# GpSimd's weight additions in quarters of 128 columns: a delta-rule attention and a gated layer on one core

## The chip, the core and the metric

The kernel runs on one NeuronCore of a Trainium2 chip. Five engines work side by side, each through its own queue in order: TensorE (PE, matrix products into PSUM), VectorE (DVE), ScalarE (ACT), GpSimd (POOL), and SyncE (SP), which here issues nearly all transfers. They meet only through semaphores. SBUF is the on-chip memory, PSUM the memory that PE writes. The metric is device time in microseconds (us) of one execution.

## The reference: what is computed

```python
state = np.zeros((B, H, D, D), dtype=np.float32)      # B, H, S, D = 4, 8, 768, 48
for t in range(S):
    kt, vt, bt = (k_n[:, :, t], v[:, :, t], beta[:, :, t, None])
    y[:, :, t] = np.einsum('bhd,bhde->bhe', q[:, :, t], state)
    v_old = np.einsum('bhde,bhd->bhe', state, kt)
    state = state + bt[:, :, :, None] * np.einsum('bhd,bhe->bhde', kt, vt - v_old)
...
h = x @ w_in            # x is y as 3072 x 384, w_in 384 x 2048
g = h * np.cos(h)
return (g @ w_out).astype(np.float32)                 # w_out 2048 x 384
```

`k_n` is `k` divided by its norm. All inputs and the output are fp32.

## The kernel before

The sequence of 768 steps is cut into 24 units of 32 steps. Within a unit, the recurrence becomes a triangular solve: PE transposes k and q (`turn`, L594), forms the products of keys with keys and queries (`gram`, L625), the triangular matrix is inverted, PE multiplies the right side by the inverse (`solve`, L897), and updates the state (`update`, L920, added by DVE at L928). For the first four units the inverse is made by elimination of 16x16 halves: PE spreads rows (`rows`, L707), and L727 and L734 multiply and subtract. Units 0 and 1 are eliminated by DVE, units 2 and 3 together by GpSimd. ACT then puts the result in place (`unfold`, L742), and PE uses it in two halves (`solve_half` and `between`, both L864). From unit 4 on the inverse is made on GpSimd by substitution (`invert`, L797 and L804), goes out through DRAM (L808) and comes back (L817). k's norms are a power on GpSimd (L541), scaled on DVE (L552 to L557).

Two units give 64 steps of 4 batches, that is 256 tokens, for the gated layer. The first two pairs use plain products (`hidden`, L980, of 12 matmuls of 128x128x128; `output`, L1181), later ones a scheme with fewer products (L1158, L1246) whose weight sums are formed from the same weights.

The weights are used in a reduced form that is prepared on the chip. `w_in` is cut into twelve blocks of 128 rows by 512 columns (`narrows[0]` to `narrows[11]`: four column groups, three row groups each), `w_out` into sixteen of 128 by 384. Each block t passes through one of six stages in `in_sum` and `w_sum` (t modulo 6): a load by SP (L489), two passes on ACT that split each word (L497, L499), two on DVE (L503 with two operands in SBUF, L508 with one), and an addition of 32-bit integers on GpSimd (`narrow_add`, L512) that writes the block in its final place. SP may load block t + 6 when the addition of block t is done; a hidden product waits for the additions of the three blocks that it reads, an output product for those of `w_out`.

The order of the work is written out by hand: every piece is a task with an engine, dependencies and buffers (`add(key, engine, ...)`), and `Order.LINE` lists the numbers of all tasks in the order in which they are emitted. `Order.OTHER` names the tasks that run on the second of two possible engines. Every engine thus has a fixed order; there is no scheduler. On GpSimd, the additions stand in this order: blocks 2, 0, 1 in one train, then 3, later 5, 4, 6, each between scalings of v (`weigh`, L582), then 7; 10 and 8 stand inside the elimination of units 2 and 3, 9 and 11 after it, with additions of `w_out` blocks around them.

Small filler matmuls (`heat`, L1194) stand on PE in the first 65 us.

Of the kernel before, what the change touches and what calls it, by code (L numbers as in the profile page):

```python
# [12 lines left out]
U32 = mybir.dt.uint32  # L13
ALU = mybir.AluOpType
# [35 lines left out]
class Order:  # L50

    OTHER = {
        ('weigh', 0, 0), ('unfold', 0), ('weigh', 0, 1), ('fold', 1), ('unfold', 1),
        ('weigh', 1, 0), ('fold', 2), ('weigh', 1, 1), ('unfold', 2), ('unfold', 3),
        ('right', 4, 0), ('left', 1, 2, 0), ('x_sum', 2, 'd'), ('x_sum', 2, 'n'),
        ('x_sum', 2, 'm'), ('x_sum', 2, 'e'), ('x_sum', 2, 'k'), ('x_sum', 2, 'g'),
        ('x_sum', 2, 'i'), ('x_sum', 2, 'l'), ('x_sum', 2, 'f'), ('x_sum', 2, 'h'),
        ('x_sum', 2, 'b0'), ('left', 2, 2, 0), ('x_sum', 3, 'd'), ('x_sum', 3, 'n'),
        ('x_sum', 3, 'm'), ('x_sum', 3, 'e'), ('x_sum', 3, 'k'), ('x_sum', 3, 'g'),
        ('x_sum', 3, 'i'), ('x_sum', 3, 'l'), ('x_sum', 3, 'f'), ('x_sum', 3, 'h'),  # L60
        ('x_sum', 3, 'b0'), ('left', 3, 1, 0), ('left', 3, 4, 1), ('left', 3, 3, 0),
        ('x_sum', 4, 'd'), ('x_sum', 4, 'n'), ('x_sum', 4, 'm'), ('x_sum', 4, 'e'),
        ('x_sum', 4, 'k'), ('x_sum', 4, 'g'), ('x_sum', 4, 'l'), ('x_sum', 4, 'f'),
        ('x_sum', 4, 'h'), ('x_sum', 4, 'b0'), ('left', 4, 4, 0), ('left', 4, 3, 0),
        ('left', 4, 3, 1), ('x_sum', 5, 'd'), ('x_sum', 5, 'm'), ('x_sum', 5, 'e'),
        ('x_sum', 5, 'i'), ('x_sum', 5, 'f'), ('x_sum', 5, 'h'), ('left', 5, 2, 0),
        ('left', 5, 4, 0), ('left', 5, 4, 1), ('left', 5, 3, 0), ('x_sum', 6, 'd'),
        ('x_sum', 6, 'e'), ('x_sum', 6, 'l'), ('x_sum', 6, 'f'), ('x_sum', 6, 'h'),
        ('x_sum', 6, 'b0'), ('left', 6, 2, 1), ('left', 6, 4, 0), ('left', 6, 3, 0),
        ('x_sum', 7, 'd'), ('x_sum', 7, 'n'), ('x_sum', 7, 'm'), ('x_sum', 7, 'g'),  # L70
        ('x_sum', 7, 'i'), ('x_sum', 7, 'h'), ('left', 7, 1, 0), ('left', 7, 2, 0),
        ('left', 7, 2, 1), ('left', 7, 4, 0), ('left', 7, 3, 1), ('x_sum', 8, 'd'),
        ('x_sum', 8, 'm'), ('x_sum', 8, 'e'), ('x_sum', 8, 'k'), ('x_sum', 8, 'f'),
        ('x_sum', 8, 'h'), ('x_sum', 8, 'b0'), ('left', 8, 4, 1), ('left', 8, 3, 0),
        ('x_sum', 9, 'n'), ('x_sum', 9, 'e'), ('x_sum', 9, 'k'), ('x_sum', 9, 'i'),
        ('x_sum', 9, 'b0'), ('left', 9, 2, 0), ('left', 9, 1, 1), ('left', 9, 4, 0),
        ('left', 9, 4, 1), ('left', 9, 3, 0), ('left', 9, 3, 1), ('x_sum', 10, 'd'),
        ('x_sum', 10, 'n'), ('x_sum', 10, 'e'), ('x_sum', 10, 'g'), ('x_sum', 10, 'l'),
        ('x_sum', 10, 'f'), ('x_sum', 10, 'h'), ('x_sum', 10, 'b0'), ('left', 10, 1, 0),
        ('left', 10, 1, 1), ('left', 10, 4, 0), ('left', 10, 3, 0), ('x_sum', 11, 'f'),  # L80
        ('x_sum', 11, 'b0'), ('left', 11, 1, 0), ('left', 11, 2, 0), ('left', 11, 2, 1),
        ('left', 11, 4, 0), ('left', 11, 4, 1),
# [139 lines left out]
def kernel(  # L222
# [287 lines left out]
    def narrow_add(t):  # L510
        w = narrows[t][0].bitcast(U32)
        nc.gpsimd.tensor_tensor(out=w, in0=w, in1=words.pop(t)[:, :, 0], op=ALU.add)  # L512
# [1315 lines left out]
```

## Time and profile before

| | us |
|---|---|
| median of 3 runs | 644.84 (644.37 to 646.28) |
| the profiled execution's own time | 644.59 |
| its span, first to last instruction | 642.8 |
| PE busy | 613.6 (95%) |
| DVE busy | 505.4 (79%) |
| POOL busy | 447.9 (70%) |
| ACT busy | 263.3 (41%) |

The profile gives for each engine its busy time, for each instruction its start and length, and for idle time the event that ended it. Groups of instructions are named by line of the kernel, engine and operation, then the tile written and the tiles read, and the shape as partitions x elements. In a timeline, the first column is the start in us from the span's begin and the second the length; `[3.61 <-DVE u_half L882]` says that the engine stood idle for 3.61 us before it, until an instruction of DVE at L882. Like instructions in a row are merged (x3). The granted clock is TensorE's, as a share of full speed. The spans of instructions on POOL are rough.

### The profile page before, as it was taken

The numbers are of one execution on the slowest core, as the hardware profiler recorded it, in microseconds if no ns is written. First come the engines' busy times: TensorE is split into PE (matmuls) and PEld (weight loads), VectorE is DVE, ScalarE is ACT, GpSimd is POOL, SyncE is SP. The second block draws the span as 40 slices with busy tenths as digits, with TensorE's granted clock in tenths as the row PEclk, the third lists the DMA queues.
The fourth block names the chain that finished last, engine by engine and source line by source line (L and its number), as shares of the span: only waits on it lengthen the run. The fifth ranks groups of instructions, "written<-read, shape, count | busy, mean of one in ns | idle before, by whom it ended". The sixth has DMA issues, their size and how long they took to land.

```text
span 642.8 us, 28246 instructions
## 1 busy us (share of the span) xinstructions
PE 613.6 (95%) x12316; PEld 572.7 (89%) x12316; DVE 505.4 (79%) x955; ACT 263.3 (41%) x467; POOL 447.9 (70%) x783
## 2 busy tenths in 40 slices
PE   5677999999999999999998999999999999999997
PEld 4566888886999989999998999999999999999997
DVE  7896887599999888789788778777778867556582
ACT  3535565822233631533523533622633433435340
POOL 4465899888888788787888886885897874152032
PEclk9677999999999999999999999999999999999999
DMA  6884475554453542635535404425304202000000
GB/s 122 217 215 133 102 197 140 123 93 70 75 96 51 100 76 40 115 64 99 89 42 98 86 7 84 74 53 101 67 2 85 51 2 34 28 2 26 2 25 25
DMA packets 202924, 50.01 MB, mean 78 GB/s; under 512 B 194544, under 2 KB 197760, under 8 KB 202800
## 3 DMA queue, kind: packets, MB, share of 16 engines
q1 hardware_dynamic: 201536, 47.82, 37.5%
q8 instruction: 97, 1.59, 1.1%
q10 hardware_dynamic: 1088, 0.20, 0.2%
q0 software_dynamic: 176, 0.18, 0.2%
q14 instruction: 27, 0.22, 0.1%
HBM read 38.19 MB, written 9.96 MB: 75 GB/s over the span
## 4 chain that ended last, share of the span: by engine, by line
PE 87%; DVE 7%; DMA 1%; issue 1%; POOL 1%; ACT 1%; SPq 0%; DVEq 0%; POOLq 0%
PE p_out L1246 29%; PE p_h L1158 28%; PE p_h L980 7%; PE p_kq L834 4%; PE p_out L1181 3%; PE p_u L897 3%; PE p_g L625 3%; PE p_s L920 3%; PE p_kq L937 3%; PE p_o L1246 2%; PE p_z L956 1%; DVE rows L734 1%; PE p_t L594 1%; DVE rows L727 1%; DVE g_ffn L1175 1%
## 5 line engine op out<-in xcount | busy, mean ns | idle before, releaser
L797 POOL TENSOR_TENSOR part<-z,gb 128x126 f32<-128x126 f32 (+22 forms) x310 | 138.8, 448 | 39.9 <-DMA gb<-g_dr 7.9
L804 POOL TENSOR_TENSOR z<-z,part 128x126 f32<-128x126 f32 (+22 forms) x310 | 145.8, 470 | 24.3
L1246 PE MATMUL p_out<-w_out,g_ffn 128*128 128x192 f32 x672 | 121.6, 329 | 2.0 <-DVE o L1298 1.8
L1246 PEld LDWEIGHTS p_out<-w_out,g_ffn 128*128 128x128 f32 x672 | 107.8, 190 | 3.7 <-issue 2.2
L1037 ACT ACTIVATE turns<-turns,halfpi 128x512 f32<-128x512 f32 x96 | 68.4, 720 | 78.7 <-DVE turns L1028 78.3
L1262 POOL TENSOR_TENSOR g_ffn<-g_ffn 128x512 f32<-128x512 f32 x37 | 49.0, 1329 | 67.3 <-DVE g_ffn L1040 46.0
L1246 PE MATMUL p_out<-w_sum,g_ffn 128*128 128x192 f32 x496 | 90.1, 329 | 0.4 <-DVE o L1298 0.4
L1158 PE MATMUL p_h<-x_sum,w_in 128*128 128x128 f32 x640 | 83.0, 277 | 0.3 <-DVE g_ffn L1175 0.3
L1246 PEld LDWEIGHTS p_out<-w_sum,g_ffn 128*128 128x128 f32 x496 | 79.5, 190 | 1.4 <-DVE o L1298 0.6
L1158 PEld LDWEIGHTS p_h<-x_sum,w_in 128*128 128x128 f32 x640 | 77.8, 192 | 1.7 <-DVE g_ffn L1175 0.6
L1021 ACT ACTIVATE turns<-g_ffn,quarter_turn 128x512 int32<-128x512 f32 x70 | 49.2, 719 | 59.8 <-DVE g_ffn L1175 38.9
L1175 DVE TENSOR_TENSOR g_ffn<-g_ffn,p_h 128x512 f32<-128x512 f32 x80 | 54.1, 679 | 24.6 <-PE p_h L1158 23.6
L1028 DVE SCALAR_TENSOR_TENSOR turns<-g_ffn,turns 128x512 f32<-128x512 f32 x70 | 55.8, 805 | 15.1 <-ACT turns L1021 14.9
L1040 DVE TENSOR_TENSOR g_ffn<-turns,g_ffn 128x512 f32<-128x512 f32 x70 | 50.9, 736 | 12.7 <-ACT turns L1037 12.6
L1158 PE MATMUL p_h<-x_sum,in_sum 128*128 128x128 f32 x400 | 54.0, 278 | 0.3 <-issue 0.3
L1158 PEld LDWEIGHTS p_h<-x_sum,in_sum 128*128 128x128 f32 x400 | 49.3, 191 | 1.5 <-issue 0.4
L980 PE MATMUL p_h<-x_ffn,w_in 128*128 128x128 f32 x384 | 48.3, 285 | 0.0
L980 PEld LDWEIGHTS p_h<-x_ffn,w_in 128*128 128x128 f32 x384 | 45.7, 198 | 1.0 <-issue 0.2
L1262 DVE TENSOR_TENSOR g_ffn<-g_ffn 128x512 f32<-128x512 f32 x51 | 44.3, 872 | 1.6 <-PE p_out L1246 1.5
L541 POOL TENSOR_TENSOR knrm<-ksum,halves 128x16 f32<-128x16 f32 (+1 forms) x14 | 38.8, 2768 | 9.0 <-DVE ksum L529 7.9
L1298 DVE SCALAR_TENSOR_TENSOR o<-p_out,o 128x192 f32<-128x192 f32 x74 | 25.0, 350 | 24.5 <-PE p_out L1246 23.8
L1170 ACT COPY p_h<-p_h 128x512 f32<-128x512 f32 x40 | 23.0, 574 | 48.9 <-PE p_h L1158 33.6
(145 smaller groups left out, 1052.9 us busy)
## 6 DMA issues: line engine op xcount, KB each, us to landing
gb<-g_dr SPq DMA_DIRECT2D x20, 256.0 KB, 4.1
vp<-in_v_dram SPq DMA_DIRECT2D x96, 48.0 KB, 3.0
in_sum<-in_moe_w_out_dram SPq DMA_DIRECT2D x12, 384.0 KB, 3.3
out_dram<-o SPq DMA_DIRECT2D x23, 192.0 KB, 2.5
in_sum<-in_moe_w_in_dram SPq DMA_DIRECT2D x8, 512.0 KB, 5.3
kp<-in_k_dram SPq DMA_DIRECT2D x128, 24.0 KB, 2.2
z_dr<-z SPq DMA_DIRECT2D x10, 256.0 KB, 3.6
zt<-z_dr SPq DMA_DIRECT2D x80, 32.0 KB, 2.4
```

The source lines that it names most:

```text
L541: nc.gpsimd.tensor_tensor(out=scales[m][2][:, part], in0=sums[m, part.start][:, 0:n], in1=halves[:, 0:n], op=ALU.pow,)
L797: nc.gpsimd.tensor_tensor(out=part, in0=z[:, 0:rows, j, None].to_broadcast(shape), in1=a[:, j, None, j + 1 :].to_broadcast(shape), op=ALU. ...
L804: nc.gpsimd.tensor_tensor(out=behind, in0=behind, in1=part, op=ALU.subtract)
L980: nc.tensor.matmul(p_h[:, i], w_in[:, t, (4 * k + i) * 128 : (4 * k + i + 1) * 128], xts[p][:, t, unit * 128 : (unit + 1) * 128], start=(i ...
L1021: nc.scalar.activation(turns[p, f], hidden_of(p, f), AF.Identity, bias=quarter_turn, scale=TURN)
L1028: nc.vector.scalar_tensor_tensor(out=r, in0=hidden_of(p, f), scalar=TURN, in1=t, op0=ALU.mult, op1=ALU.subtract,)
L1037: nc.scalar.activation(r, r, AF.Sin, bias=halfpi, scale=2.0 * math.pi)
L1040: nc.vector.tensor_tensor(out=place(p, f), in0=step_of(rests.pop((p, f)), f), in1=step_of(hidden_of(p, f), f), op=ALU.mult,)
L1158: nc.tensor.matmul(p_h[:, e], in_block(*w)[:, e], x_of(p, b), start=new and e == 0, stop=True, skip_group_check=True,)
L1175: nc.vector.tensor_tensor(out=part_of(p, to), in0=part_of(p, one), in1=part_of(p, two), op=op)
L1246: nc.tensor.matmul(p_o, left(p, part, a)[:, e % 4], right(e, b), start=(e == 0), stop=(e == FT // 2 - 1), skip_group_check=True,)
L1262: either(("left", p, x, s), nc.vector, nc.gpsimd).tensor_tensor(out=left(p, s, to), in0=left(p, s, one), in1=left(p, s, two), op=op)
```

## The change

Each addition of a `w_in` block on GpSimd becomes four additions of 128 columns, in the order of the columns, directly behind one another. The sixteen additions of `w_out` blocks stay whole. The last quarter keeps the key of the old task, so what depends on the block in the task list still depends on its last quarter; in the instructions, each matmul that reads a quarter waits for that quarter. In `LINE` 36 numbers are added and the others renumbered; `OTHER` holds the same 120 keys in another sequence. Leaving the quarters out, the order on every engine is the same as before.

```diff
     OTHER = {
...
     LINE = """
...
-    def narrow_add(t):
-        w = narrows[t][0].bitcast(U32)
-        nc.gpsimd.tensor_tensor(out=w, in0=w, in1=words.pop(t)[:, :, 0], op=ALU.add)
+    PIECES = 4
+
+    def narrow_add(t, piece, pieces):
+        w, lo = narrows[t][0].bitcast(U32), words[t][:, :, 0]
+        n = narrows[t][2] // pieces
+        cols = slice(piece * n, piece * n + n)
+        nc.gpsimd.tensor_tensor(out=w[:, cols], in0=w[:, cols], in1=lo[:, cols], op=ALU.add)
+        if piece == pieces - 1:
+            words.pop(t)
...
         add(("shift", t), "DVE", 1.4 * c, lambda: narrow_shift(t), [("split", t)])
-        add(("add", t), "POOL", 1.45 * c, lambda: narrow_add(t), [("shift", t)],
+        deps, pieces = [("shift", t)], PIECES if t < 12 else 1
+        for i in range(pieces - 1):
+            add(("part", t, i), "POOL", 0.5, lambda i=i: narrow_add(t, i, pieces), deps)
+            deps = [("part", t, i)]
+        add(("add", t), "POOL", 1.45 * c / pieces, lambda: narrow_add(t, pieces - 1, pieces), deps,
             due=W_IN + 2 * t if t < 12 else W_OUT + 2 * (t - 12))
```

More of the change, by code (lines that the diff above doesn't have):

```diff
@@ L52 @@
     OTHER = {
[L53 to L82, printed above, removed]
+        ('weigh', 0, 0), ('unfold', 1), ('left', 7, 4, 0), ('x_sum', 8, 'h'), ('left', 9, 3, 0),
@@ new lines @@
+        ('x_sum', 4, 'b0'), ('x_sum', 11, 'f'), ('left', 7, 3, 1), ('left', 5, 4, 0),
+        ('x_sum', 3, 'e'), ('x_sum', 2, 'l'), ('x_sum', 7, 'd'), ('left', 4, 3, 1),
+        ('left', 4, 4, 0), ('x_sum', 3, 'm'), ('x_sum', 3, 'k'), ('fold', 2), ('left', 6, 3, 0),
+        ('unfold', 3), ('x_sum', 7, 'n'), ('left', 1, 2, 0), ('unfold', 0), ('x_sum', 7, 'h'),
+        ('x_sum', 5, 'e'), ('left', 9, 4, 1), ('x_sum', 4, 'l'), ('x_sum', 6, 'f'),
+        ('left', 7, 1, 0), ('x_sum', 3, 'b0'), ('x_sum', 5, 'm'), ('x_sum', 10, 'f'),
@@ new lines @@
+        ('x_sum', 2, 'd'), ('x_sum', 9, 'n'), ('left', 7, 2, 1), ('x_sum', 7, 'i'),
+        ('x_sum', 8, 'f'), ('x_sum', 2, 'n'), ('x_sum', 4, 'g'), ('left', 4, 3, 0),
+        ('x_sum', 2, 'h'), ('x_sum', 4, 'd'), ('x_sum', 10, 'g'), ('unfold', 2),
+        ('x_sum', 9, 'i'), ('x_sum', 3, 'l'), ('left', 10, 4, 0), ('x_sum', 4, 'n'),
+        ('left', 2, 2, 0), ('x_sum', 2, 'i'), ('x_sum', 4, 'h'), ('left', 9, 1, 1),
+        ('left', 3, 3, 0), ('x_sum', 6, 'e'), ('left', 5, 4, 1), ('x_sum', 11, 'b0'),
@@ new lines @@
+        ('left', 10, 1, 0), ('left', 3, 1, 0), ('x_sum', 10, 'e'), ('x_sum', 3, 'd'),
+        ('x_sum', 8, 'e'), ('left', 10, 3, 0), ('x_sum', 3, 'n'), ('x_sum', 7, 'g'),
+        ('x_sum', 6, 'b0'), ('x_sum', 3, 'h'), ('x_sum', 8, 'm'), ('left', 5, 2, 0),
+        ('left', 11, 1, 0), ('x_sum', 8, 'k'), ('x_sum', 2, 'f'), ('x_sum', 5, 'd'),
+        ('left', 3, 4, 1), ('x_sum', 10, 'b0'), ('weigh', 1, 1), ('left', 11, 2, 1),
+        ('x_sum', 3, 'i'), ('x_sum', 8, 'b0'), ('x_sum', 5, 'h'), ('x_sum', 4, 'f'),
@@ new lines @@
+        ('x_sum', 2, 'g'), ('left', 8, 3, 0), ('left', 6, 2, 1), ('x_sum', 6, 'l'),
+        ('x_sum', 4, 'k'), ('left', 11, 4, 1), ('x_sum', 5, 'i'), ('x_sum', 7, 'm'),
+        ('left', 9, 2, 0), ('x_sum', 10, 'l'), ('x_sum', 9, 'e'), ('fold', 1),
+        ('left', 10, 1, 1), ('weigh', 0, 1), ('weigh', 1, 0), ('x_sum', 2, 'e'),
+        ('left', 11, 2, 0), ('left', 5, 3, 0), ('left', 9, 3, 1), ('x_sum', 9, 'k'),
+        ('x_sum', 3, 'f'), ('left', 9, 4, 0), ('x_sum', 6, 'd'), ('left', 8, 4, 1),
@@ L83 @@
+        ('x_sum', 2, 'm'), ('x_sum', 2, 'k'), ('x_sum', 10, 'd'), ('left', 7, 2, 0),
+        ('x_sum', 4, 'e'), ('x_sum', 6, 'h'), ('left', 11, 4, 0), ('x_sum', 9, 'b0'),
+        ('x_sum', 5, 'f'), ('x_sum', 8, 'd'), ('x_sum', 10, 'n'), ('x_sum', 3, 'g'),
+        ('x_sum', 2, 'b0'), ('x_sum', 10, 'h'), ('x_sum', 4, 'm'), ('right', 4, 0),
+        ('left', 6, 4, 0),
     }
     LINE = """
[98 rows of a table removed]
[99 rows of a table added]
 """
```

197 rows, old and new, of the table LINE are left out of this document.

## The prediction

> **What bounds the kernel now.** I read the page first (shares, the chain that ended last), then busy time by stage, and then, for the stage that stood out, the timelines of the vector engine (DVE), GpSimd (POOL) and TensorE (PE).
>
> ```profile
> PE 613.6 (95%) x12316; PEld 572.7 (89%) x12316; DVE 505.4 (79%) x955; ACT 263.3 (41%) x467; POOL 447.9 (70%) x783
> ...
> PE 87%; DVE 7%; DMA 1%; issue 1%; POOL 1%; ACT 1%; SPq 0%; DVEq 0%; POOLq 0%
> ```
>
> Busy time by stretch (the columns after the length are PE, PE weight loads, DVE, ACT, POOL, each busy us with instructions; then the granted clock):
>
> ```profile
> 30.00:35.00 5.00, 1.39 (x65) 1.23 (x64) 4.76 (x10) 0.82 (x2) 3.22 (x3) 0.50 0.83 227
> ...
> 45.00:50.00 5.00, 2.33 (x70) 1.32 (x69) 4.83 (x9) 0.37 (x1) 3.89 (x4) 0.97 0.82 208
> 50.00:55.00 5.00, 3.36 (x74) 3.19 (x75) 4.30 (x18) 2.69 (x7) 0.56 (x1) 0.50 0.73 233
> ```
>
> PE is busy for 613.6 of 642.8 us and carries 87% of the chain, so a microsecond counts only where PE stands still. The long idle stretches lie early: 1.39 of 5 us busy from 30 to 35 and 2.33 from 45 to 50, while DVE is busy 4.76 and 4.83. There DVE is the bound, and PE follows it. From 50 to 55 PE's granted clock is 0.50. What PE waits for, in its timeline (start, length, idle before and releaser):
>
> ```profile
> 33.77 1.50 PE L897 MATMUL p_u<-u_half,halves_z 32*32 32x48 f32 x64 [3.61 <-DVE u_half L882]
> ...
> 46.21 1.13 PE L1194 MATMUL p_out<-halfpi 128*128 128x512 f32 x2
> 51.64 1.34 PE L625 MATMUL p_g<-kq_t 48*32 48x64 f32 x64 [4.31 <-DVE rows L727]
> 52.91 4.66 PE L980 MATMUL p_h<-x_ffn,w_in 128*128 128x128 f32 x24
> ...
> 67.74 2.84 PE L980 MATMUL p_h<-x_ffn,w_in 128*128 128x128 f32 x24
> ...
> 81.24 0.88 PE L864 MATMUL p_w<-rhs,halves_z 32*32 32x48 f32 x64
> ...
> 97.33 2.75 PE L1181 MATMUL p_out<-w_out,g_ffn 128*128 128x384 f32 x8
> ...
> 136.51 0.88 PE L897 MATMUL p_u<-rhs,zt 32*32 32x48 f32 x64
> ```
>
> PE stands 3.61 us for a DVE write (L882) and 4.31 us for DVE's elimination rows. From 52.91 on these rows carry no idle time, so an earlier start there travels to the end unless a later wait appears. Now DVE and POOL side by side in that stretch, DVE first:
>
> ```profile
> 26.11 0.17 DVE L552 TENSOR_TENSOR knrm<-knrm,tiny 128x8 f32<-128x8 f32 x1 [1.18 <-POOL knrm L541]
> ...
> 29.50 1.27 DVE L552 TENSOR_TENSOR knrm<-knrm,tiny 128x8 f32<-128x8 f32 x1
> 30.81 1.20 DVE L554 TENSOR_TENSOR krec<-knrm 128x8 f32<-128x8 f32 x1
> ...
> 32.29 0.96 DVE L557 TENSOR_TENSOR bs<-bt,krec 128x8 f32<-128x8 f32 x1
> 33.17 0.54 DVE L882 TENSOR_TENSOR u_half<-vp,p_v 128x384 f32<-128x384 f32 x1
> ...
> 36.87 0.68 DVE L503 SCALAR_TENSOR_TENSOR in_sum<-in_sum 128x512 uint32<-128x512 uint32 x1
> ...
> 38.66 1.14 DVE L503 SCALAR_TENSOR_TENSOR w_sum<-w_sum 128x512 uint32<-128x512 uint32 x1
> ...
> 43.32 0.24 DVE L734 TENSOR_TENSOR rows<-rows 128x80 f32<-128x80 f32 x1
> 43.60 0.23 DVE L727 TENSOR_TENSOR rows<-rows,p_r 128x72 f32<-128x72 f32 x1
> 43.86 1.02 DVE L734 TENSOR_TENSOR rows<-rows 128x72 f32<-128x72 f32 x1
> ...
> 45.58 1.79 DVE L503 SCALAR_TENSOR_TENSOR in_sum<-in_sum 128x512 uint32<-128x512 uint32 x1
> ...
> 47.87 1.27 DVE L734 TENSOR_TENSOR rows<-rows 128x56 f32<-128x56 f32 x1
> ...
> 55.35 0.54 DVE L849 TENSOR_TENSOR rhs<-vp,p_kq 128x384 f32<-128x384 f32 x1
> ```
>
> ```profile
> 29.47 3.75 POOL L512 TENSOR_TENSOR w_in<-w_in,in_sum 128x512 uint32<-128x512 uint32 x3
> 37.96 1.29 POOL L512 TENSOR_TENSOR w_in<-w_in,in_sum 128x512 uint32<-128x512 uint32 x1 [4.74 <-DVE w_in L508]
> ...
> 43.50 1.29 POOL L512 TENSOR_TENSOR w_in<-w_in,w_sum 128x512 uint32<-128x512 uint32 x1
> ...
> 45.54 1.29 POOL L512 TENSOR_TENSOR w_in<-w_in,w_sum 128x512 uint32<-128x512 uint32 x1
> 47.79 1.28 POOL L512 TENSOR_TENSOR w_in<-w_in,in_sum 128x512 uint32<-128x512 uint32 x1 [0.96 <-DVE w_in L508]
> ...
> 72.08 1.74 POOL L512 TENSOR_TENSOR w_in<-w_in,w_sum 128x512 uint32<-128x512 uint32 x1
> 73.78 1.47 POOL L512 TENSOR_TENSOR w_in<-w_in,in_sum 128x512 uint32<-128x512 uint32 x1
> ...
> 79.00 0.25 POOL L734 TENSOR_TENSOR rows<-rows 128x16 f32<-128x16 f32 x1
> ...
> 93.79 1.99 POOL L512 TENSOR_TENSOR w_out<-w_out,in_sum 128x384 uint32<-128x384 uint32 x2
> ```
>
> L552 on 128x8 takes 0.17 us at 26.11; at 29.50 it takes 1.27, and L554 and L557, of the same size, 1.20 and 0.96. Three GpSimd additions of 3.75/3 = 1.25 us each run from 29.47. L552 ends at 30.77 and L554 at 32.01, each at an addition's end (29.47 + 1.25 = 30.72, then 31.97); L557 ends at 33.25, as does the third. So a DVE operation with two operands in SBUF waits for the whole GpSimd instruction beside it, and gets its turn between two instructions even where the next addition already stands in the queue. L734 at 43.86 (1.02, its neighbour of 43.32 0.24), L503 at 45.58 (1.79 against 0.68) and L734 at 47.87 (1.27) stand beside the additions of 43.50, 45.54 and 47.79. L727 (43.60, 0.23 beside the first of these) has one operand in PSUM and is not slowed.
>
> **The price of a quarter.** Three additions of 512 columns take 3.75, 1.25 each; two of 384 columns (93.79) take 1.99, 1.00 each: 0.25 per 128 columns and 0.25 fixed. A quarter is then 0.50, less some hundredths by which the ends in a train overlap (1.29 for one alone against 1.25); I take 0.47, between 0.31 (nothing fixed) and 0.58, the mean of GpSimd's 128x128 sums with their waits:
>
> ```profile
> L1073 POOL TENSOR_TENSOR x_sum<-x_sum,x_ffn 128x128 f32<-128x128 f32 x13 | 7.5, 580 | 5.4 <-DVE x_sum L1073 5.2
> ```
>
> Four take 1.88: 0.63 more per block, 7.6 us for twelve, all on POOL.
>
> **Part 1, the train of three additions at 29.47.** After the change L552 waits for one quarter (end 29.47 + 0.47 = 29.94), L554 for the next (30.4), the reciprocal for none, L557 for the rest of the third (30.9). L557 ends 33.25 - 30.9 = 2.35 earlier. L882 (one operand in PSUM) and p_u at 33.77 follow. Against it: the twelve quarters now last to about 35.5 (5.6 us and some turns of DVE), so four L734 and L503 of 36.87 fall beside them; each waits 0 to 0.3, five times 0.13 is 0.65. Net gain 1.7; bounds 0.8 (five full waits) and 2.35.
>
> **Part 2, the addition at 37.96.** L503 at 38.66 loses 1.14 - 0.68 = 0.46; with quarters about 0.2. Gain 0.3, bounds 0 and 0.46.
>
> **Part 3, the additions at 43.50, 45.54 and 47.79.** Lost now: 1.02 - 0.24 = 0.78, 1.79 - 0.68 = 1.11, and 1.27 - 0.24 = 1.03, in all 2.92. After it twelve quarters can each hold up one L734, for what is left of the quarter when L727 (0.23) is done: 0 to 0.24, I take 0.14, 1.65 in all. Gain 1.3, bounds 0 (twelve full waits) and 2.9. Part of the train also slides behind the last L727 that PE awaits at 51.64, as DVE reaches it earlier; it stays in the upper bound.
>
> Sum on DVE: 1.7 + 0.3 + 1.3 = 3.3 us, bounds 0.8 and 5.7. All of it lies on the path, since DVE is full in these stretches and PE waits for it at 33.77 and 51.64.
>
> **What becomes late.** POOL has a longer line, and what is queued behind must be followed. The second addition, ending at 31.97, frees the stage that SP's weight load fills:
>
> ```profile
> 32.02 0.35 SPq L489 DMA_DIRECT2D in_sum<-in_moe_w_in_dram  x1
> ```
>
> It now ends near 33.5, and SP's later loads move by 1.5 us. DVE shifts that block only at 45.58, so this costs 0. The scalings of v that stand between POOL's additions are first read on the path by L849 at 55.35: 0. Of the other blocks, two (72.08, 73.78) lie inside GpSimd's elimination, which ends at 79.00 + 0.25 = 79.25; they add 1.3 there, perhaps 1.6 with DVE's turns. ACT unfolds the result and PE uses it at 81.24:
>
> ```profile
> 79.28 0.69 ACT L742 ACTIVATE halves_z<-rows,consts 128x128 f32<-128x128 f32 x2 [1.15 <-POOL rows L734]
> ```
>
> 79.28 + 0.69 = 79.97, a slack of 1.27: I put 0.3 us of new PE wait here, bounds 0 and 0.8. Two more feed a hidden product in which PE reads quarter i of the third block only at its third, sixth, ninth and twelfth matmul: the later end is met by later need, 0. The two w_out additions of 93.79 end at 95.78, wanted at 97.33 at the earliest and the second of them only by the product's last quarter 2 us later; POOL is then about 2.5 late: 0. GpSimd's substitution comes back to SBUF by SP's loads
>
> ```profile
> 129.24 2.15 SPq L817 DMA_DIRECT2D zt<-z_dr  x4
> ```
>
> ```profile
> zt<-z_dr SPq DMA_DIRECT2D x80, 32.0 KB, 2.4
> ```
>
> which land at 129.24 + 2.15 + 2.4 = 133.8, for p_u at 136.51: 2.7 us of slack against those 2.5, 0.
>
> PE itself gets more semaphore waits in its first hidden products, on quarters long done: 0.
>
> Forecast: 3.3 - 0.3 = 3.0 us. The profiled execution took 644.59 (span 642.8 and 1.8 around it), 0.25 under the median of 644.84. 644.6 - 3.0 = 641.6.
>
> **The rivals.** (a) The clock stays up. From the end of the filler at 46.21 + 1.13 = 47.34 PE idles 4.31 us and comes back at clock 0.50; the product of 52.91 takes 4.66, its like at 67.74 takes 2.84. Of my 3.3 us, 2.0 are earned ahead of the filler and 1.3 behind it, which leaves a gap of 3.0. If that no longer drops the clock, the product gains 4.66 - 2.84 = 1.8 and p_g of 51.64 in the same ratio 0.5, 2.3 together: 639.3. L849 ends at 55.89, 1.7 before that product ends at 57.57, so DVE would let most of it pass. The trace shows one gap that drops the clock, 4.31; 3.0 lies nearer to it than to none, so 0.22. [...]
>
> (b) The wait only changes its shape: twelve small waits for one long one in parts 1 and 3, at the low bounds. 0.8 less 0.3 at 81.24: 644.1, no change to be told. The shortness of DVE's operations there (0.2 to 0.28) speaks for it, the three L55x rows against.
>
> (c) Slower, by POOL's line: DVE takes a turn between all quarters in the elimination, so that the blocks at 72.08 and 73.78 swell. They already stretch to 1.74 and 1.47. It decides from 0.88 us per quarter on: then two blocks grow by 2 x (3.5 - 1.25) = 4.5, the slack of 1.27 and the gain of 3.3 together. At 1.2 per quarter they grow by 7.1, and the result is 644.6 - 3.3 + 7.1 - 1.3 = 647.1. Against it: a turn of DVE adds its own length, mostly 0.2 to 0.7 here, and not every quarter meets one.
>
> (d) The port is not handed over between quarters, so the change does not do what it says: each of seven waits in parts 1 to 3 grows by up to 0.63, I take 3.4 us in all, and 644.6 + 3.4 = 648.0. The ends at 30.77 and 32.01 speak against it. [...]
>
> **How the numbers follow.** A difference of 0.3%, 1.9 us, is about what a measurement of this kernel can tell from none. Forecast 0.45 (its own range, gain 1.9 to 4.4: 640.2 to 642.7), (a) 0.22, (b) 0.15, (c) 0.11, (d) 0.07. Faster: 0.45 + 0.22 = 0.67; same: 0.15; slower: 0.18. The range runs from 638.6, (a) with 0.7 us of part 3's upper bound, up to 646.0; (d) and most of (c) are left out.
>
> **What would show it.** In DVE's timeline the three operations at 29.50 end near 30.9, each under 0.5 us; L882 starts near 30.8 and p_u near 31.4. The quarters start 0.47 apart where DVE is quiet. PE's p_g of 51.64 starts near 48.3, and the ACT unfold near 76.5 to 77. The clock in the first hidden product decides on (a). Wrong would be: quarters over 0.6 us, L552 still over 1 us, or a PE wait of over 1 us at the p_w of 81.24, the product of 97.33 or the p_u of 136.51.

## The result, and the profile after

The changed kernel took 642.0 us in the median of 20 runs (636.75 to 647.18), the kernel before 645.1 beside it (642.14 to 647.97, also 20). The two medians differ by 3.1 us. The ratio is taken from fast runs alone, without the one slow run of 647.18: 0.9936, 95% interval 0.992 to 0.9953, that is 0.64% faster, 4.1 us. The profiled execution took 642.55 us with a span of 640.8, 2.0 under the one of before. Line numbers in the changed kernel are 1 higher than before up to L509 and 7 higher from L548 on; the addition is L517. In the kernels of the experiments they are the old ones up to L509 and 6 higher behind the addition (3 higher in the one called bands).

Busy time and the chain that ended last, then the stretches that stood out (length, then PE, PE weight loads, DVE, ACT, POOL, each with instructions; then granted clock, DMA share, GB/s):

```profile
PE 614.1 (96%) x12316; PEld 571.8 (89%) x12316; DVE 501.0 (78%) x955; ACT 263.0 (41%) x467; POOL 455.9 (71%) x819
...
PE 87%; DVE 4%; SPq 2%; issue 2%; DMA 1%; ACT 1%; POOL 1%; POOLq 0%; DVEq 0%
```

```profile
30.00:35.00 5.00, 3.36 (x72) 3.09 (x72) 4.61 (x14) 1.57 (x3) 4.79 (x12) 0.50 0.76 210
35.00:40.00 5.00, 4.06 (x101) 3.31 (x101) 5.00 (x9) 3.86 (x7) 3.15 (x6) 0.52 1.06 332
40.00:45.00 5.00, 1.90 (x109) 1.61 (x115) 4.65 (x16) 1.67 (x4) 5.00 (x5) 1.00 0.58 134
45.00:50.00 5.00, 5.00 (x150) 3.17 (x147) 3.17 (x12) 2.16 (x5) 4.71 (x11) 0.66 0.47 99
```

DVE has 4.4 us less to do, POOL 8.0 more. DVE's share of the chain falls from 7% to 4%. PE does 3.36 instead of 1.39 us of work from 30 to 35 and fills 45 to 50 wholly, but from 40 to 45 it now stands still, and "issue" (time in which PE waited for nothing that the profile shows) rises from 1% to 2%. The timelines of DVE, POOL and PE:

```profile
29.69 0.44 DVE L559 TENSOR_TENSOR knrm<-knrm,tiny 128x8 f32<-128x8 f32 x1
30.17 0.39 DVE L561 TENSOR_TENSOR krec<-knrm 128x8 f32<-128x8 f32 x1
...
30.82 0.17 DVE L564 TENSOR_TENSOR bs<-bt,krec 128x8 f32<-128x8 f32 x1
...
31.81 0.53 DVE L741 TENSOR_TENSOR rows<-rows 128x120 f32<-128x120 f32 x1
...
42.84 0.69 DVE L504 SCALAR_TENSOR_TENSOR in_sum<-in_sum 128x512 uint32<-128x512 uint32 x1
```

```profile
29.65 5.13 POOL L517 TENSOR_TENSOR w_in<-w_in,in_sum 128x128 uint32<-128x128 uint32 x12
...
48.06 1.70 POOL L517 TENSOR_TENSOR w_in<-w_in,in_sum 128x128 uint32<-128x128 uint32 x4
...
67.61 2.98 POOL L517 TENSOR_TENSOR w_in<-w_in,w_sum 128x128 uint32<-128x128 uint32 x4
```

```profile
31.64 1.50 PE L904 MATMUL p_u<-u_half,halves_z 32*32 32x48 f32 x64 [1.75 <-DVE u_half L889]
...
40.83 0.92 PE L841 MATMUL p_kq<-st,kq_t 48*32 48x48 f32 x77
44.85 0.69 PE L841 MATMUL p_kq<-st,kq_t 48*32 48x48 f32 x51 [3.10 <-issue]
...
49.70 0.98 PE L632 MATMUL p_g<-kq_t 48*32 48x64 f32 x64
50.61 2.94 PE L987 MATMUL p_h<-x_ffn,w_in 128*128 128x128 f32 x24
...
77.90 0.88 PE L871 MATMUL p_w<-rhs,halves_z 32*32 32x48 f32 x64
...
144.42 0.55 PE L963 MATMUL p_z<-consts,y 128*128 128x128 f32 x3 [0.59 <-ACT y L955]
```

The same p_z in the kernel before has no wait:

```profile
147.10 0.49 PE L956 MATMUL p_z<-consts,y 128*128 128x128 f32 x3
```

The waits that the change was about are gone as forecast: 1.27, 1.20 and 0.96 became 0.44, 0.39 and 0.17, p_u starts 2.31 earlier (counted from the start of the train of additions), L504 takes 0.69 instead of 1.79, and the wait of 4.31 ahead of p_g is gone. Two things are new: PE stands 3.10 us in the middle of a group of 128 matmuls with no semaphore in sight, and it waits 0.59 at the p_z of 144.42 for a copy by ACT.

### The profile page after: what moved, and what is told of

Its sections match the earlier page's. It is cut to its first block, busy times and chain, and to the rows that moved or that the text cites. A ratio compares the mean times of both kernels' runs of the same rounds, so it can differ in the third digit from the quotient of the medians.

```text
span 640.8 us, 28283 instructions
## 1 busy us (share of the span) xinstructions
PE 614.1 (96%) x12316; PEld 571.8 (89%) x12316; DVE 501.0 (78%) x955; ACT 263.0 (41%) x467; POOL 455.9 (71%) x819
## 4 chain that ended last, share of the span: by engine, by line
PE 87%; DVE 4%; SPq 2%; issue 2%; DMA 1%; ACT 1%; POOL 1%; POOLq 0%; DVEq 0%
PE p_out L1253 29%; PE p_h L1165 28%; PE p_h L987 7%; PE p_kq L841 4%; PE p_s L927 3%; PE p_kq L944 3%; PE p_u L904 3%; PE p_g L632 3%; PE p_out L1188 3%; SPq L358 2%; PE p_o L1253 2%; PE p_z L963 1%; PE p_r L714 1%; DMA qp<-in_q_dram 1%; DVE g_ffn L1182 1%
## 5 line engine op out<-in xcount | busy, mean ns | idle before, releaser
L811 POOL TENSOR_TENSOR z<-z,part 128x126 f32<-128x126 f32 (+22 forms) x310 | 144.3, 465 | 24.3
L1165 PEld LDWEIGHTS p_h<-x_sum,in_sum 128*128 128x128 f32 x400 | 49.4, 191 | 1.3 <-DVE g_ffn L1182 0.3
L987 PE MATMUL p_h<-x_ffn,w_in 128*128 128x128 f32 x384 | 46.6, 278 | 0.0
L548 POOL TENSOR_TENSOR knrm<-ksum,halves 128x16 f32<-128x16 f32 (+1 forms) x14 | 39.0, 2788 | 8.4 <-DVE ksum L536 7.2
L987 PEld LDWEIGHTS p_h<-x_ffn,w_in 128*128 128x128 f32 x384 | 44.0, 192 | 0.9
```

The source lines that it names most:

```text
L548: nc.gpsimd.tensor_tensor(out=scales[m][2][:, part], in0=sums[m, part.start][:, 0:n], in1=halves[:, 0:n], op=ALU.pow,)
L811: nc.gpsimd.tensor_tensor(out=behind, in0=behind, in1=part, op=ALU.subtract)
L987: nc.tensor.matmul(p_h[:, i], w_in[:, t, (4 * k + i) * 128 : (4 * k + i + 1) * 128], xts[p][:, t, unit * 128 : (unit + 1) * 128], start=(i ...
L1165: nc.tensor.matmul(p_h[:, e], in_block(*w)[:, e], x_of(p, b), start=new and e == 0, stop=True, skip_group_check=True,)
```

## The experiments

The kernels of the experiments are the kernel before with another `narrow_add` that issues the parts of one addition directly behind one another (with four parts for all twelve blocks this is the changed kernel's order on every engine). Two are made otherwise: "bands" has a `narrow_add` of its own, and "before, loads moved" keeps the old one. The new `narrow_add`:

```diff
     def narrow_add(t):
-        w = narrows[t][0].bitcast(U32)
-        nc.gpsimd.tensor_tensor(out=w, in0=w, in1=words.pop(t)[:, :, 0], op=ALU.add)
+        w, lo = narrows[t][0].bitcast(U32), words.pop(t)[:, :, 0]
+        n = narrows[t][2] // PIECES.get(t, 1)
+        for c in range(0, narrows[t][2], n):
+            nc.gpsimd.tensor_tensor(
+                out=w[:, c : c + n], in0=w[:, c : c + n], in1=lo[:, c : c + n], op=ALU.add
+            )
```

Starts differ from run to run before anything that was changed: the train of additions begins between 28.38 and 29.92. So the table gives distances between events of one profile: from the start of POOL's train of three additions to p_u, from p_u to p_s, from p_s to the p_g that stood at 51.64, from there to the p_z that stood at 147.10, and the rest of the span.

| kernel | train to p_u | p_u to p_s | p_s to p_g | p_g to p_z | p_z to end | ratio to before |
|---|---|---|---|---|---|---|
| before | 4.30 | 3.33 | 14.54 | 95.46 | 495.7 | |
| after | 1.99 | 4.34 | 13.72 | 94.72 | 496.4 | 0.9936 [0.9920, 0.9953] |
| quarters in the train only | 1.98 | 4.34 | 14.93 | 95.19 | 496.9 | 0.9979 [0.9955, 1.0003] |
| quarters in the middle four | 4.31 | 3.33 | 11.04 | 95.03 | 496.2 | 0.9945 [0.9914, 0.9976] |
| quarters in the late five | 4.30 | 3.33 | 14.55 | 98.18 | 495.8 | 1.0012 [0.9994, 1.0030] |
| quarters in the first seven | 1.99 | 4.34 | 11.10 | 96.20 | 500.1 | 0.9946 [0.9914, 0.9978] |
| halves | 2.65 | 3.97 | 12.84 | 95.39 | 495.5 | 0.9939 [0.9913, 0.9965] |
| eighths | 1.72 | 3.42 | 12.15 | 101.27 | 498.6 | 1.0001 [0.9978, 1.0025] |
| after, loads moved | 1.98 | 4.36 | 11.76 | 97.39 | 495.8 | 0.9954 [0.9928, 0.9980] |
| before, loads moved | 4.31 | 3.33 | 14.54 | 96.35 | 497.2 | 0.9992 [0.9965, 1.0018] |
| after, once more | 1.99 | 4.35 | 11.05 | 95.94 | 497.2 | 0.9943 [0.9917, 0.9969] |
| first seven, loads moved | 1.99 | 4.34 | 11.04 | 96.55 | 497.5 | 0.9952 [0.9922, 0.9981] |
| halves in seven, loads moved | 2.66 | 3.97 | 13.10 | 96.62 | 497.8 | 0.9948 [0.9917, 0.9978] |
| bands | 3.20 | 6.03 | 14.63 | 96.11 | 497.5 | (one run, 649.23 against 646.39) |

### The parts of the change, one at a time

Quarters in the train alone:

```diff
+    PIECES = {t: 4 for t in (2, 0, 1)}
```

> Quarters in the train of three additions at 29.47 alone (blocks 2, 0 and 1); all other additions whole. Port theory (a DVE operation with two operands in SBUF waits for the GpSimd instruction beside it and no longer): the three L55x operations of DVE end near 30.9, u_half starts near 31.0 and PE's p_u near 31.6 instead of 33.77; four L741/L734 behind it lose about 0.25 each (1.0), so DVE is about 1.1 ahead from 36 on; the long waits at the later additions (0.8, 1.1, 1.0 us) are still there, and PE's p_g of 51.64 starts near 50.5. Whole kernel 1.1 us faster than before with a cold clock in the first hidden product, up to 2.5 if the shorter gap keeps it up. Supply theory (PE runs out of instructions at about its 590th matmul, because the next 16 KB come behind the loads): PE shows an idle of 1 to 3 us with no semaphore near 41 to 44, which here costs nothing, as DVE's rows are waited for anyway. Rival, that the gain of the change comes from the later additions: p_u early, but the end moves under 0.5.

The first step is exact: 1.98 instead of 4.30, and 1.01 given back by the four rows (L740 here) before p_s. Counted from the train, p_g came 0.9 earlier, and PE idled 1.38 with no semaphore ahead of 43.79. The ratio's interval includes 1: the train alone is worth 0.2%, if anything.

Quarters in the middle four alone:

```diff
+    PIECES = {t: 4 for t in (3, 5, 4, 6)}
```

> Quarters in the four additions at 37.96, 43.50, 45.54 and 47.79 alone (blocks 3, 5, 4, 6). Port theory: L55x stay at 1.27, 1.20, 0.96 and p_u at 33.8; of the 0.46 + 2.92 us that DVE loses beside these four, 1.0 to 1.5 stay, so p_g of 51.64 starts 1.9 to 2.4 earlier, near 49.5. The gap ahead of it falls from 4.31 to about 2.2; if the clock then stays up, the first hidden product takes 2.9 instead of 4.66 and the kernel gains 3.5, otherwise 2. No supply stall of over 0.5 us near 41 to 44, since PE passes its 508th matmul no earlier than before. Rival (waits only change shape): under 0.5 us.

The middle is worth 3.50 us from p_s to p_g, more than expected and more than the train. DVE's timeline:

```profile
39.75 0.86 DVE L503 SCALAR_TENSOR_TENSOR w_sum<-w_sum 128x512 uint32<-128x512 uint32 x1
...
42.92 0.69 DVE L503 SCALAR_TENSOR_TENSOR in_sum<-in_sum 128x512 uint32<-128x512 uint32 x1
43.52 0.69 DVE L508 TENSOR_SCALAR w_in<-w_in 128x512 uint32<-128x512 uint32 x1
...
45.81 0.48 DVE L740 TENSOR_TENSOR rows<-rows 128x32 f32<-128x32 f32 x1
...
47.07 0.45 DVE L740 TENSOR_TENSOR rows<-rows 128x24 f32<-128x24 f32 x1
```

The L503 of 42.92, which took 1.79, is no longer slowed; the other four rows and one more L508 of 0.69 are what this stretch still loses. In the kernel before, some that the prediction did not count were slowed too, and these stand beside GpSimd's scalings of v (L582), which the change leaves whole:

```profile
39.73 1.05 DVE L508 TENSOR_SCALAR w_in<-w_in 128x512 uint32<-128x512 uint32 x1
...
45.17 0.49 DVE L734 TENSOR_TENSOR rows<-rows 128x64 f32<-128x64 f32 x1
...
49.41 0.50 DVE L734 TENSOR_TENSOR rows<-rows 128x48 f32<-128x48 f32 x1
```

```profile
39.21 1.28 POOL L582 TENSOR_TENSOR vp<-vp,knrm 128x384 f32<-128x384 f32 x1
...
44.75 0.83 POOL L582 TENSOR_TENSOR vp<-vp,knrm 128x384 f32<-128x384 f32 x1
...
49.02 0.83 POOL L582 TENSOR_TENSOR vp<-vp,knrm 128x384 f32<-128x384 f32 x1
```

Against 0.42, 0.24 and 0.20 unslowed, that is 0.63 + 0.25 + 0.30 = 1.2 beside the 3.4 that the prediction has; 4.6 lost before. With quarters 0.18 + 0.27 + 0.27 + 0.29 + 0.27 = 1.3 is left. The difference, 3.3, is nearly the 3.50 that p_g gained. But not all of it is a shorter wait. POOL's timeline of this run:

```profile
40.02 3.34 POOL L547 TENSOR_TENSOR knrm<-ksum,halves 128x16 f32<-128x16 f32 x1
43.34 2.06 POOL L516 TENSOR_TENSOR w_in<-w_in,w_sum 128x128 uint32<-128x128 uint32 x4
```

Counted from the train, this addition starts 0.9 later than before, and DVE reaches the L503 of 42.92 1.6 earlier. So the three operations that took 1.02, 0.49 and 1.79 before now start while POOL computes the power of the norms (L547), ahead of the additions: 0.78 + 0.25 + 1.11 = 2.1 of the 3.3. Beside the first addition in quarters DVE lost less, and POOL was done with it later (2.35 instead of 1.29); after that DVE passes in front of the next ones.

Quarters in the late five alone:

```diff
+    PIECES = {t: 4 for t in (7, 10, 8, 9, 11)}
```

> Quarters in the five additions from 53 us on alone (blocks 7, 10, 8, 9, 11). Nothing differs up to 53 us. POOL's line is 5 x 0.55 = 2.8 us longer (2 to 3 with waits), while PE is no earlier, so what POOL feeds comes later against PE: theory of the longer line: PE waits 0 to 0.8 at the p_w of 81.24, and 0.8 to 2.5 us at the p_z of 147.1 by way of GpSimd's substitution, SP's queue of loads and the scalar engine behind the zt load; kernel slower by 0.8 to 2.5 us. Rival (POOL's line has slack all the way, the loss in the changed kernel at 144 us is of another cause): same time, no wait over 0.3 at either place.

The waits came where the theory put them: 0.38 at the p_w of 81.44 and 1.03 at the p_z, which started 2.7 later than before, counted from the train. Of this, 0.65 belongs to the first hidden product, which took 5.31 against 4.66 before and 2.94 at the full clock. The chain behind the wait at the p_z is seen in ACT's queue, where y stands two places behind ksq, and in SP's:

```profile
147.33 0.84 ACT L530 ACTIVATE ksq<-kp 128x768 f32<-128x768 f32 x1 [5.15 <-DMA zt<-z_dr]
...
148.65 0.47 ACT L954 COPY y<-p_kq 128x384 f32<-128x384 f32 x1
```

```profile
132.04 1.96 SPq L823 DMA_DIRECT2D zt<-z_dr  x4
...
140.67 4.65 SPq L357 DMA_DIRECT2D kp<-in_k_dram  x8
145.36 1.91 SPq L823 DMA_DIRECT2D zt<-z_dr  x4
```

```profile
149.17 0.55 PE L962 MATMUL p_z<-consts,y 128*128 128x128 f32 x3 [1.03 <-ACT y L954]
```

The profile puts ksq's wait down to a load of zt, GpSimd's substituted block, but ksq reads kp, and it started at 147.33, before any of the zt loads issued from 145.36 on had landed (the first did at 147.75). It waited for the last of the eight loads of kp, issued up to 145.32. These stand in SP's order behind the earlier loads of zt (132.04, before at 129.24), and SP can issue those only when GpSimd has the block ready. So a late GpSimd holds up loads that it has nothing to do with.

The time is 0.12% longer, with an interval that includes no change. So the five late ones have a cost in the trace, some 2 us at the p_z without that product's share, and at most 0.3% in the time.

Quarters in the first seven only:

```diff
+    PIECES = {t: 4 for t in (0, 1, 2, 3, 4, 5, 6)}
```

> Quarters in the first seven additions (up to 48 us), the five later ones whole. Theory: up to 53 us as in the changed kernel (L55x end near 30.9, p_u 31.6, PE idle about 3 us with no semaphore near 42 to 45, p_g without a wait near 49.7, first hidden product near 2.9 us); POOL then is 2.8 us less late, the wait of 0.59 at the p_z of 144.42 is gone and the stages at 150 us are 0.8 us earlier than in the changed kernel: ratio to before near 0.992, 0.1% under the changed kernel's 0.9936. Rival: the loss after 140 us is not POOL's, and ratio and waits are the changed kernel's.

As expected there is no wait at the p_z, which started at 142.59, 4.0 earlier than before, counted from the train. The idle without a semaphore was 1.47 instead of 3. But the profiled run gave all of the gain back behind the p_z, and the ratio cannot be told from the changed kernel's. PE's timeline and the granted clock show where:

```profile
161.57 0.24 PE L840 MATMUL p_kq<-st,kq_t 48*32 48x48 f32 x3 [1.94 <-issue]
...
349.26 4.52 PE L1252 MATMUL p_out<-w_out,g_ffn 128*128 128x192 f32 x16 [1.82 <-DVE o L1304]
```

```profile
162.00:164.00 2.00, 2.00 (x48) 1.83 (x39) 1.29 (x4) 0.00 (x0) 1.70 (x4) 0.50 0.04 8
```

An idle of 1.94 with no semaphore (0.21 at this place before), then half the clock; and half the clock again from 349.7 on, behind a wait of 1.82. That wait stands in all fourteen profiles of this case, to 0.01. In twelve the product behind it takes 2.84 (the clock stays at 1.00 in the kernel before), in two it takes 4.52 (the clock falls, to 0.50 from 350 to 352 in this run). The second of the two is the kernel before with two loads moved, of which more below; here it stands under the kernel before itself:

```profile
350.25 2.84 PE L1246 MATMUL p_out<-w_out,g_ffn 128*128 128x192 f32 x16 [1.82 <-DVE o L1298]
```

```profile
351.32 4.52 PE L1246 MATMUL p_out<-w_out,g_ffn 128*128 128x192 f32 x16 [1.82 <-DVE o L1298]
```

So this is a loss of 1.68 that falls on one execution and not on another, whatever the additions do.

### The size of a part, and what is shared

Halves and eighths of all twelve:

```diff
+    PIECES = {t: 2 for t in (0, 1, 2, 3, 4, 5, 6, 7, 8, 9, 10, 11)}
```

> All twelve additions in halves of 256 columns. Price of a piece from the changed kernel: a whole addition 1.29, four quarters alone 1.70, so 0.14 per extra instruction and 0.71 for a half. Port theory: in the train the L55x operations each wait for up to one half, ending near 30.2, 30.9 and (after the reciprocal) 31.6, so p_u near 32.3, between before (33.77) and quarters (31.64). Beside the later additions an L741 or L504 loses up to 0.5. POOL's line is 12 x 0.14 = 1.7 us longer than before instead of 8 as measured with quarters (4 us without DVE's turns), so the wait at the p_z of 144.42 is under 0.3. Ratio to before 0.993 to 0.997. Rival (what counts is that DVE gets in at all, not the length of the piece): L55x as short as with quarters, 0.2 to 0.4.

```diff
+    PIECES = {t: 8 for t in (0, 1, 2, 3, 4, 5, 6, 7, 8, 9, 10, 11)}
```

> All twelve additions in eighths of 64 columns. Price of a piece 1.29 + 7 x 0.14 = 2.25 for eight, 0.28 each. Port theory: L55x take 0.2 to 0.3 and u_half starts near 30.7, 0.3 earlier than with quarters; but each L741 in a train still loses up to 0.28, and more of them lie beside one. POOL's line is 5 to 7 us longer than with quarters, and PE waits 2 to 5 us more at the p_w of 78, the p_z of 144 or in the first hidden products: ratio to before 0.996 to 1.004, slower than the changed kernel by 2 to 5 us. Rival (POOL's line has slack): the time of the changed kernel within 1 us.

DVE's operations beside the train of additions, the first two with halves, then the first with eighths:

```profile
28.55 0.72 DVE L558 TENSOR_TENSOR knrm<-knrm,tiny 128x8 f32<-128x8 f32 x1
29.31 0.66 DVE L560 TENSOR_TENSOR krec<-knrm 128x8 f32<-128x8 f32 x1
```

```profile
29.20 0.31 DVE L558 TENSOR_TENSOR knrm<-knrm,tiny 128x8 f32<-128x8 f32 x1
```

The first operation, 0.17 when nothing holds it up, takes 1.27, 0.72, 0.44, 0.31 us with parts of 512, 256, 128 and 64 columns: the wait goes with the length of the part beside it. A half is 1.42/2 = 0.71, a quarter 1.70/4 = 0.43, an eighth 2.25/8 = 0.28. Halves cannot be told from quarters in time: the train is 0.66 worse, p_u to p_s 0.37 better, and the twelve additions are shorter, 19.2 in all against 24.1 with quarters and 16.3 whole. The wait at the p_z was expected under 0.3 and was 0.60 all the same. Eighths are best up to p_s, but POOL's line came back later, by 1.52 ahead of a hidden product and by 1.45 at the p_z. In this profile the clock also fell behind the first of these, to 0.50 from 74.9 on, and that product took 4.58, where its like takes 2.84 or 2.94 at the full clock:

```profile
74.32 4.58 PE L986 MATMUL p_h<-x_ffn,w_in 128*128 128x128 f32 x24 [1.52 <-ACT row_copies L724]
```

Nothing is left of the gain: the ratio is 1.0001.

Bands of 64 partitions, two per block, in the train:

```diff
+        n = 64 if t in (2, 0, 1) else 128
+        for p in range(0, 128, n):
+            b = slice(p, p + n)
+            nc.gpsimd.tensor_tensor(out=w[b], in0=w[b], in1=lo[b], op=ALU.add)
```

> The additions of blocks 2, 0 and 1 in two bands of 64 partitions by all 512 columns instead of one instruction: two instructions per block, each as long as a whole addition (1.25 by theory, as the columns set the time). Port theory: DVE waits for the length of the instruction beside it, so L55x take 1.2 to 1.3, 1.2 and about 1.0 as in the kernel before, u_half starts near 33.2 and p_u near 33.8; and the train lasts 7.5 us, so that one to four L740 behind it lose up to 1 us each. The kernel is slower than before by 2 to 5 us. Rival (what counts is the number of hand-overs between instructions, or fewer elements per instruction): L55x under 0.8 as with halves of columns.

```profile
29.95 1.27 DVE L555 TENSOR_TENSOR knrm<-knrm,tiny 128x8 f32<-128x8 f32 x1
31.25 0.17 DVE L557 TENSOR_TENSOR krec<-knrm 128x8 f32<-128x8 f32 x1
```

```profile
29.92 8.03 POOL L515 TENSOR_TENSOR w_in<-w_in,in_sum 64x512 uint32<-64x512 uint32 x6
```

Half the elements, but 8.03/6 = 1.34 us each, and DVE's first operation takes 1.27 again, 0.55 more than beside a half by columns. So neither twice as many instructions nor fewer elements shorten the wait; a shorter instruction does. One step was off: the second operation slipped in between two bands (0.17), and p_u came at 33.12. The third took 0.91, and behind the train p_u to p_s grew to 6.03. The time of the one run, 649.23 against a median of 646.39, lies in the expected 2 to 5 us, but the runs of the kernel before beside it reach from 643.72 to 653.21, so it shows little.

### The idle without a semaphore

PE's instructions come over a DMA queue of their own, in 97 packets of 16 KB for 24,632 matmuls and weight loads, 254 each; the twelfth packet starts when 1530 matmuls have started, in the changed kernel as in the one before. The trace lists them by stretch (queue: packets, MB, share of 16 engines). From 30 to 41 us the changed kernel's DMA engines served loads only, and the next packet started at 42.26:

```profile
q1 hardware_dynamic: 3230, 3.05, 91.5%
```

```profile
q8 instruction: 1, 0.02, 3.1%
```

(The first line is the whole list of queues from 30 to 41, the second its part on instructions from 42.2 to 44.5.) In the four kernels below in which loads were moved out of its way, this packet starts when 494 to 507 matmuls have started; here PE passed 505 at 38.7, 3.6 us ahead of the packet. It ended at 43.4, and PE went on at 44.85. To test it, the loads of blocks 7 and 8 (512 KB each) went behind two groups of smaller loads in SP's order, in the changed kernel and in the kernel before:

```diff
-2042 2034 184 2048 2055 94 129 44 2038 70 45 46 2059 2063 125 208 2052 71 47 2045 185 237 2049 2056
+2042 2034 184 2048 2055 94 129 44 2038 70 45 46 125 208 2059 2063 2052 71 47 2045 185 237 2049 2056
```

> The changed kernel, with SP's loads of weight blocks 7 and 8 (512 KB each, issued at 35.75) put behind the loads of v and q that follow them; nothing else moved. Supply theory: the DMA queues are then free near 39, the 16 KB of PE's instructions that came at 42.35 come before 41, and the idle of 3.10 us without a semaphore ahead of 44.85 is gone (under 0.5). The filler then ends near 45 instead of 49.8, p_g of 49.70 waits for DVE's rows instead, and the first hidden product starts 1.5 to 2.5 us earlier at the full clock: ratio to before near 0.990, some 2 us under the changed kernel. Clock: the window at half clock from 46.8 to 50.2 disappears. Rival (the stall is not of the loads but of PE's own queue): 3 us of idle at the same place.

> The kernel before, with the same two loads moved. Supply theory: its packet of instructions comes a little earlier, but PE passes the place at 43.7 without a stall, and DVE's rows set the p_g of 51.64: same time within 0.5 us, ratio 0.999 to 1.001. So the loads cost only where PE comes early. Rival (the loads disturb DVE or POOL too): a gain of over 1 us here as well.

With the loads moved, the changed kernel has its packet between 38 and 40, and PE no idle there; it waits for DVE instead:

```profile
q8 instruction: 1, 0.02, 3.0%
```

```profile
47.46 1.16 PE L631 MATMUL p_g<-kq_t 48*32 48x64 f32 x64 [2.16 <-DVE rows L733]
48.55 4.57 PE L986 MATMUL p_h<-x_ffn,w_in 128*128 128x128 f32 x24
```

The mechanism holds: the stall is one of supply, and loads ahead of the packet make it. The two further kernels with the loads moved (below) have no such idle either, while the kernels with the train in quarters and the loads in their old place idled 1.38, 1.47, 1.71 and 3.10. In the kernel before the same move changed no distance up to p_g, as forecast. But the two further microseconds did not come. The idle only changed its place: PE now stood 2.16 for DVE ahead of p_g, the clock fell to 0.50 from 49.4 to 52.9, and the first hidden product took 4.57 instead of 2.94. In the changed kernel's own profile the clock fell as well, behind the idle of 3.10, but from 46.6 to 50.0, and so on the filler and p_g and not on the product. The p_z started at 144.85, with a wait of 1.18 for y, and the ratio is 0.9954.

### Both losses taken away

A group with the changed kernel once more as its yardstick, then the first seven in quarters and the first seven in halves, both with the loads moved:

```diff
+    PIECES = {t: 4 for t in (0, 1, 2, 3, 4, 5, 6, 7, 8, 9, 10, 11)}
...
+    PIECES = {t: 4 for t in (0, 1, 2, 3, 4, 5, 6)}
...
+    PIECES = {t: 2 for t in (0, 1, 2, 3, 4, 5, 6)}
```

> The changed kernel once more, as the yardstick of this group: ratio to before 0.992 to 0.996. Supply theory: the packet of instructions that PE asks for at its 505th matmul starts 1 to 4 us after that, as DMA is full, and PE idles 0.5 to 3 us with no semaphore near 42 to 45. Theory of the longer line: PE waits for the scalar engine's y at a p_z near 144.4 to 144.9.

> Quarters in the first seven additions, five whole, and the loads of weight blocks 7 and 8 behind the loads of v and q. Theory: both losses of the changed kernel are gone: no idle without a semaphore of over 0.5 near 42 to 45, and no wait over 0.3 for y at the p_z near 143; the first hidden product starts 4.5 to 5.5 earlier than before, and that still stands at 140 us. Ratio to before 0.990 to 0.993, 1 to 2 us under the changed kernel. Rival (the later stages take it back whatever the early ones do): ratio of the changed kernel.

> Halves in the first seven additions, five whole, and the same two loads moved. Theory: DVE's three operations end 0.5 later than with quarters, but POOL's line is only 7 x 0.14 = 1 us longer than before and DVE's turns fewer: u_half starts near 31.0, first hidden product 4 to 5 earlier than before, no wait for y at the p_z near 143. Ratio to before 0.990 to 0.994. Rival (quarters needed): 1 us behind the quarters of this group.

The yardstick repeated the result, 0.9943, with an idle of 1.71 for the packet; its p_z stood at 142.82 with a wait of 0.19, earlier than expected, so that wait too is not the same in every run. The second had what the theory promised and was not measurably faster: no idle near 42, p_g 4.8 earlier counted from the train, no wait at the p_z, and 0.9952, with an interval that just reaches the expected 0.993. PE's timeline shows where part of it went:

```profile
53.18 0.88 PE L870 MATMUL p_w<-rhs,halves_z 32*32 32x48 f32 x64 [1.68 <-DVE tt L754]
```

Behind the product, which now has the full clock (2.94 us), DVE is late again by 1.68, then ACT by 1.52 at 58.10. So the rival, that later stages take back what is gained beyond some 3 to 4 us, fits better than my theory. The halves came to their first hidden product 2.3 earlier than before, counted from the train, and not 4 to 5: PE waited 3.08 for DVE ahead of p_g, and the product took 5.06 instead of the 2.94 of the full clock. Their ratio is 0.9948 all the same. The intervals of these kernels overlap that of the changed kernel, so none of them can be told from it.

## Why the prediction was right, and where its parts were not

- **What bounds the kernel** held: where DVE's long waits went, PE started earlier by the same amount.
- **The price of a quarter** (0.47): 0.43 alone and in the train, where 5.13 includes DVE's turns. The fixed part is (1.70 - 1.29)/3 = 0.14 per extra instruction, not 0.25, but DVE's turns in the elimination (2.98 for the first block) brought what POOL has more to do to 8.0 us, against 7.6 forecast. The sign "quarters over 0.6" came true in that one block (0.75 each), without the loss that it was to announce.
- **Part 1**: gross gain 2.35 forecast, 4.30 - 1.99 = 2.31 measured. Given back 0.65 forecast, 4.34 - 3.33 = 1.01 measured: all four L741 waited 0.25, over half a quarter each. Net 1.3 instead of 1.7.
- **Parts 2 and 3**: 1.6 forecast, 3.4 to 3.5 measured in four kernels with the middle in quarters (11.04 to 11.10 against 14.54), 2.8 in a fifth (11.76), and only 0.8 in the changed kernel's own profile, where the supply set p_g. The place was right and the size not, in two ways. Operations beside the scalings of v were left out of the loss (1.2 us). And the sum counts twelve shorter waits, whereas 2.1 of the gain is DVE passing in front of the additions altogether; the prediction has that only as a remark to its upper bound. It hangs on some tenths of a microsecond: in the changed kernel with the loads moved, the addition began 0.46 ahead of this L503 and not 0.42 behind it, and the L503 took 0.97 instead of 0.69.
- **The new wait that no rival had** is the supply of PE's instructions: 3.10 us in that profile, 1.71 in its repetition.
- **Rival (a)**, the clock: the first hidden product took 2.94 instead of 4.66, and p_w behind it stood 4.0 earlier where p_g stood 1.9 earlier. So what (a) counts came true, but not as it argues. It needs a gap of 3.0 ahead of p_g that leaves the clock up; this profile has no gap there, its clock fell behind the supply's idle of 3.10, and it was back at 1.00 just as the product began. That is luck. Where there was a gap of 3.08, in the halves with the loads moved, the product took 5.06 and not 2.94: the clock fell, as the forecast had it. Where p_g was earlier still, DVE held the next p_w, by 1.68: my check that DVE would let the gain pass looked at L849 and not at the operation behind it.
- **What becomes late**: the forecast 0.3 at p_w did not appear (77.90 has no wait). The transfers at p_u of 136.51 had slack as said. What failed is that only zt's own reader was followed, and not the loads that stand behind zt in SP's order. Those of kp, which ACT needs ahead of its copy of y, cost 0.59 here, 0.19 in the repetition and 1.03 with the late quarters alone. Counted from the train they were issued 1.6 earlier than before, but PE was ready for y 3.45 earlier. GpSimd's line is not the whole cause: the wait was 0.46 with the train alone and 0.60 with halves.
- **Rivals (b), (c), (d)**: the train's first wait of 0.44 rules out (d), and the 3.5 us in the middle rule out (b). A quarter took 2.98/4 = 0.75 in the elimination, under the 0.88 from which (c) decides; at eighths its kind of loss did eat the whole gain.
- **The sum**: 641.6 from 644.6 is 0.47% under, the edge of the measured 0.47% to 0.80%. It came out as more gain (1.3, up to 3.5, and the clock) and more loss (supply, y, DVE behind the product) than the 3.3 and 0.3 on record. That the total agrees is not evidence for its terms; the distances are.

What stays open: from the p_z to the end, fourteen profiles took 495.5 to 500.1 us. The kernel before has 495.7 and, with nothing but two loads moved, 497.2; that 1.5 is the clock's fall at 351, worth 1.68. Idles at the p_kq near 160 to 167 (none to 1.94) make another part. Why the clock falls behind the same wait in one execution and not in another, and why the kernels with halves or quarters in the middle, whose profiles reach the p_z 1.3 to 4.3 us earlier (counted from the train), all end 3 to 4 us earlier, was not tested.

## What to carry to other kernels

Where a short operation on one engine waits for the whole length of a neighbour's instruction, cut the neighbour into parts along the dimension that sets its length (here the columns: 0.71 us with half of them, 1.34 with half the partitions), and only as far as its own queue has slack: halves gave here what quarters gave, within the noise, and eighths gave it all back. Ask too which of the two engines will stand in front after the cut; in the middle that was worth more than the shorter waits. Compare distances between events of one profile and not starts: up to p_s they repeated within 0.03 us where the additions were the same, while the starts moved by over 1 us; behind that they moved too, with the supply and the clock. And when PE comes early, look for what must come early with it: its instructions, the engine that feeds the next product, the loads of a later stage.

## What the hardware showed

- A DVE operation with a single operand in SBUF is slowed too: L508 on 128x512 took 1.05 instead of 0.42 beside a scaling by GpSimd, and 0.69 beside quarters, which the prediction's rule of two operands did not cover. What it is that DVE waits for, called a port in the prediction and the expectations, no run shows; measured is how long it waits, and that this is no wait for a semaphore: L552's 1.27 at 29.50 (0.17 at 26.11) is the operation's own length, with no idle before it. So the two engines do not meet through semaphores alone.
- Either engine can be the one that waits. In the train of quarters each L741 took 0.25 longer (0.53 at 31.81). Beside the quarters of 43.34 in the run with the middle four, three such rows took 0.24, 0.21 and 0.20, as without them, and the four quarters took 2.06 instead of 1.70. What decides between the two was not tested.
- PE can run dry in the middle of a group: 3.10 us at 44.85, with the packet of instructions 3.6 us late behind loads that kept the DMA engines at a share of 1.06 from 35 to 40.
- An idle of 1.5 to 2.2 us can halve the clock, for 3.5 us from 49.4 to 52.9 with the loads moved and about 3.4 at 349.7 (a loss of 1.68 at half the clock), or leave it up. It fell behind 1.52 (eighths, at 74.32), 1.94 (at 161.57), 2.16 (loads moved, ahead of p_g) and in two of fourteen profiles behind the same wait of 1.82; ahead of p_g, 1.03, 1.40, 1.75 and 1.78 left it up. So the length of the idle alone does not decide in this range. Ahead of p_g, 3.08 (halves in seven, loads moved), 4.17 (late five) and 4.31 (before) were each followed by a first hidden product of 5.06, 5.31 and 4.66, against 2.94 at the full clock.
